# Block-diagonal w_phi for the two-block projections, and a new order of steps, in a fused linear-attention and FFN kernel

## The chip, the cores and the metric

The kernel runs on one core of a Trainium2 chip. The metric is device time in microseconds (us) of one execution; lower is better. A profile is of one execution, which has a time of its own; the time of the kernel is the median of several executions without a profile. TensorE is called PE in the profile, VectorE DVE, ScalarE ACT, GpSimd POOL and SyncE SP.

## What is computed

q, k and v have the shape (8, 8, 576, 64): batch, heads, positions, head size. w_phi is 64 x 128. Attention is linear, with a feature map of exponentials, and its output goes through a feed-forward network (FFN) with a squared relu.

```python
def phi(x):
    proj = einsum('bhsd,df->bhsf', x, w_phi)
    proj = proj - max(abs(proj), axis=-1, keepdims=True)
    return concatenate([exp(proj), exp(-proj)], axis=-1)
q_p, k_p = phi(q), phi(k)
kv = einsum('bhsf,bhsd->bhfd', k_p, v)
z = sum(k_p, axis=2)
num = einsum('bhsf,bhfd->bhsd', q_p, kv)
den = einsum('bhsf,bhf->bhs', q_p, z)[..., None] + 1e-06
x = (num / den).transpose(0, 2, 1, 3).reshape(4608, 512)
out = square(maximum(x @ w_in, 0)) @ w_out     # w_in 512 x 2048, w_out 2048 x 512
```

## The kernel before

The work is two streams that PE interleaves: the attention of eight batches, and the FFN of nine chunks of 512 tokens. Chunk c is the first 512 positions of batch c; chunk 8 collects the last 64 positions of every batch. An FFN chunk starts when the attention of its batch is done, and while PE works on it, the attention of the next batch goes on.

A batch's k and q are turned so that the head size lies on partitions (kT and qT), with two heads in the two halves of the 128 partitions: 18 blocks of 128 columns. Batches 0 and 1 are turned by PE (steps Txk, Txq), the later ones by transposing DMAs that SP issues (Xxk, Xxq, L339). Sixteen blocks come in groups of four; blocks 16 and 17, the last 64 positions, are a group of two, the group with index 4.

For a group, `project` (L347 to L360, matmuls at L355) multiplies each block by w_phi, once with the lower 64 partitions and once with the upper 64. These matmuls use half of the array's rows each, so two of them run side by side; they write to two PSUM banks. The steps are Pk for keys and Pq for queries. Then DVE takes the largest magnitude (Mk at L410, Mq at L517), and ACT the exponentials (L416). Queries of batches 0 to 4 are projected a second time in transposed form (Fq, L577), with w_phi as the stationary matrix, also in half-array form, and ACT writes their exponentials (L592). From batch 5 on (LATE), ACT takes them from Pq (L536) and a DMA turns them (Xf, L544). Batch 0 has forms of its own for Pk, most Pq and Fq (`first`, L382, L510).

V (L443, DVE) scales v by the key maxima's exponentials. KV (L473, L478) multiplies key features and v. NA and NB (L607) multiply query features and KV, with a scaling by DVE between (SA, L619); then come the reciprocal (L627), the division (xo, L631), and a transposing DMA to xT or xS (Xx, L665).

F1 (L751; f1 at L762 for chunk 0) is x @ w_in, one bank of 512 tokens and four matmuls at a time. relu (L726 on ACT or L728 on DVE) and the squaring (L735, DVE or POOL) follow. F2 (L816) adds four matmuls to an output tile of 128 tokens; after four parts the tile is copied (L196 or L198, "ot") and stored (L832, L835). The very last tile, token tile 3 of chunk 8, is done in two halves of 256 columns (`last_out`, L780, copies L794 and L796, stores L803).

The order is written out. Every step is an `Op` with a sequence number; the list `ORDER` gives the order in which all of them are emitted, and so the order on each engine and DMA queue, where work is strictly first come, first served. `BASES` gives each PSUM tile its bank, `STATES` chooses between two engines for the steps that have an alternative (relu, squaring, copies, V), `GATES` names for each load from batch 2 on a step that it has to wait for, and `FILL` puts matmuls on zeros ahead of some early steps (L885). Loads are issued by POOL (L254, L262, L274, L285, L301, L307). All these are fixed numbers in the file.

Of the kernel before, what the change touches and what calls it, by code (L numbers as in the profile page):

```python
# [111 lines left out]
def kernel(  # L112
# [10 lines left out]
    nc = tc.nc  # L123
# [4 lines left out]
    P = 128  # L128
# [34 lines left out]
    wphi2 = sb("wphi2", [Fd])  # L163
    ident = sb("ident", [P])
# [67 lines left out]
    add("DVE", dve_cost(64), f_wcast, r=[("wphi_f", 0), ("wphi_f", 1)], w=["wphi2"], what="wcast")  # L232

# [83 lines left out]
    def attention(b):  # L317
# [29 lines left out]
        def project(xt, ttag, ts, what):  # L347
            g = Bank(2, "att")
            n = len(ts)
# [9 lines left out]
            return g  # L359

# [6 lines left out]
        def kgroup_ops(g):  # L367
# [41 lines left out]
            def fn():  # L409
                pin(nc.vector.tensor_reduce(  # L410
                    out=mk_view(g), in_=ps2(pj)[:, :, : n * Fd].rearrange("p e (i f) -> p e i f", f=Fd),
                    axis=AX.X, op=ALU.max, apply_absolute_value=True))
            add("DVE", dve_cost(2 * n * Fd), fn, r=[pj], w=[pj] + [("mk", s2, g, e) for e in range(2)], what="Mk")
            for sgn, dst, nm in ((1.0, kp, "kp"), (-1.0, kn, "kn")):
                def fn(dst=dst, sgn=sgn):
                    pin(nc.scalar.activation(out=dst[slot][:, :, :n, :].rearrange("p e i f -> p e (i f)"),  # L416
                                             in_=ps2(pj)[:, :, : n * Fd], func=ACT.Exp, scale=sgn))
# [84 lines left out]
        def qmax_ops(c):  # L502
# [13 lines left out]
            def fn():  # L516
                pin(nc.vector.tensor_reduce(  # L517
                    out=mqb[:, c, :, :n], in_=ps2(pj)[:, :, : n * Fd].rearrange("p e (i f) -> p e i f", f=Fd),
                    axis=AX.X, op=ALU.max, apply_absolute_value=True))
            turned = b >= LATE  # L520
            add("DVE", dve_cost(2 * n * Fd), fn, r=[pj], w=[("mq", s2, c)] + [pj] * turned, closes=None if turned else pj, what="Mq")
            if turned:
# [6 lines left out]
                for u, sgn in enumerate((1.0, -1.0)):  # L529
                    def fn(u=u, sgn=sgn):  # L530
                        i_, o = ps2(pj)[:, :, : n * Fd], qe[:, u, : 2 * n * Fd]
                        if c == 4:
                            o, i_ = o.rearrange("p (i e f) -> p e i f", e=2, f=Fd), i_.rearrange("p e (i f) -> p e i f", f=Fd)
                        else:
                            o = o.rearrange("p (e x) -> p e x", e=2)
# [26 lines left out]
        def q_ops(c):  # L562
            ts = q_ts(c)
            n = min(len(ts), 4)
            pf = Bank(2, "att")
            def fn():
                o = ps2(pf)
# [11 lines left out]
            add("PE", pe_cost(1, 0.222 * n / 4 * (2 if first and c < 4 else 1)), fn,  # L579
                r=[("qT", s2, t) for t in ts] + ["wphi2"], w=[pf], opens=pf, tiled=True, what="Fq")  # L580
# [3 lines left out]
            for sgn, dst, nm in ((1.0, qp, "qp"), (-1.0, qn, "qn")):  # L584
                def fn(dst=dst, sgn=sgn):
                    i_ = ps2(pf)[:, :, : n * P]
# [447 lines left out]
```

## Time and profile before

| | |
|---|---|
| median of 3 runs | 350.82 us (350.69 to 351.57) |
| profiled execution | 351.74 us |
| its span, first to last instruction | 350.0 us |
| PE busy | 338.1 us, 97% |
| DVE busy | 277.3 us, 79% |
| ACT busy | 224.0 us, 64% |
| POOL busy | 96.7 us, 28% |
| granted clock of PE | 1.00 in every stretch |

Busy times of PE count a matmul from its start to a modelled end, and matmuls overlap: a 512-column one lasts 379 ns in the record, and the next starts 216 ns after it. So a matmul's cost is read from start to start. In the views of groups and waits, "L751 PE MATMUL psum<-xT,win" is line 751's matmul that writes psum and reads xT and win. In a timeline row the columns are the start, the length, the engine, the line, the operation, and how many instructions the row merges; what stands in brackets is idle time before it and what ended it. In a row of stretches, the busy time of each engine is followed by its number of instructions.

### The profile page before, as it was taken

To read this page: it belongs to the slowest core of one execution; us is meant where nothing else is said; L and a number is where in the kernel's file an instruction comes from. 1 tells how busy PE (TensorE), PEld (TensorE's weight loads), DVE (VectorE), ACT (ScalarE), POOL (GpSimd) and SP (SyncE) were. 2 spreads that over 40 slices of the span, in tenths; PEclk is the share of its full clock that TensorE was granted. 3 is DMA by queue.
4 is the path that set the end of the run, shared out by engine and by line. 5 is a ranking of instruction groups with operands and counts; after the bars stand their busy time and mean duration, and the time that the engine had idled before them with its cause. 6 is when DMAs were issued, how large, how long until landed. Compare 5 with 4: busy or idle time off the path is not lost.

```text
span 350.0 us, 8421 instructions
## 1 busy us (share of the span) xinstructions
PE 338.1 (97%) x3336; PEld 192.0 (55%) x3370; DVE 277.3 (79%) x530; ACT 224.0 (64%) x422; POOL 96.7 (28%) x144
## 2 busy tenths in 40 slices
PE   7889999999999999999999999999999999999995
PEld 5669976544654655465546544555546544444453
DVE  4999998899989997899998877988867737861421
ACT  4999886599779998785886776677537400122210
POOL 8744450298607143441100470220000000000000
PEclk9999999999999999999999999999999999999999
DMA  7999999799999999999997998979595621100024
GB/s 93 174 199 201 198 98 160 154 117 148 201 170 168 111 173 134 165 131 134 181 173 133 146 221 131 179 114 150 135 190 89 133 60 67 62 0 1 32 97 113
DMA packets 124328, 46.70 MB, mean 133 GB/s; under 512 B 92800, under 2 KB 119808, under 8 KB 124288
## 3 DMA queue, kind: packets, MB, share of 16 engines
q0 software_dynamic: 45216, 18.36, 47.2%
q1 hardware_dynamic: 78752, 27.50, 41.0%
q8 instruction: 26, 0.43, 0.5%
q10 hardware_dynamic: 320, 0.30, 0.4%
q14 instruction: 14, 0.11, 0.1%
HBM read 36.77 MB, written 9.44 MB: 132 GB/s over the span
## 4 chain that ended last, share of the span: by engine, by line
PE 81%; DVE 10%; DMA 4%; issue 3%; ACT 2%; POOL 0%; DVEq 0%; ACTq 0%; POOLq 0%
PE psum L751 30%; PE psum L816 29%; PE psum L607 5%; PE psum L355 5%; PE psum L473 4%; PE psum L762 3%; DVE va L443 2%; DMA xT<-xo 2%; DMA xq<-in_q_dram 2%; DVE mq L517 2%; PE psum L577 1%; DVE mk L410 1%; DVE mk L389 1%; PE psum L780 1%; PE psum L478 1%
## 5 line engine op out<-in xcount | busy, mean ns | idle before, releaser
L816 PE MATMUL psum<-wout,h 128*128 128x512 bf16 x526 | 129.3, 379 | 2.1 <-issue 0.5
L751 PE MATMUL psum<-xT,win 128*128 128x512 bf16 x448 | 106.3, 379 | 0.7 <-DMA xT<-xo 0.7
L726 ACT ACTIVATE hr<-psum 128x512 bf16<-128x512 f32 x88 | 51.4, 599 | 51.7 <-PE psum L751 28.4
L816 PEld LDWEIGHTS <-h 128*128 128x128 bf16 x560 | 51.1, 98 | 54.9 <-issue 1.0
L751 PEld LDWEIGHTS <-win 128*128 128x128 bf16 x512 | 47.3, 98 | 54.5 <-issue 1.8
L735 DVE TENSOR_TENSOR h<-hr 128x512 bf16<-128x512 bf16 x143 | 55.7, 414 | 8.5 <-ACT hr L726 8.1
L592 ACT ACTIVATE qf<-psum 128x1024 bf16<-128x1024 f32 (+1 forms) x50 | 45.5, 936 | 11.4 <-PE psum L577 7.2
L517 DVE TENSOR_REDUCE mq<-psum 128x8 f32<-128x1024 f32 (+1 forms) x40 | 44.0, 1109 | 3.2 <-PE psum L355 2.8
L728 DVE TENSOR_SCALAR hr<-psum 128x512 bf16<-128x512 f32 x56 | 37.6, 685 | 9.4 <-PE psum L751 7.6
L410 DVE TENSOR_REDUCE mk<-psum 128x8 f32<-128x1024 f32 (+1 forms) x35 | 38.4, 1111 | 5.7 <-PE psum L355 5.3
L416 ACT ACTIVATE kp<-psum 128x1024 bf16<-128x1024 f32 (+1 forms) x35 | 32.6, 936 | 7.8 <-DVE mk L410 7.8
L607 PEld LDWEIGHTS <-qf 128*128 128x128 bf16 x640 | 28.2, 97 | 13.1 <-issue 0.9
L619 DVE TENSOR_TENSOR psum<-psum,en 128x520 f32<-128x520 f32 (+1 forms) x40 | 27.6, 699 | 6.6 <-PE psum L607 4.9
L416 ACT ACTIVATE kn<-psum 128x1024 bf16<-128x1024 f32 (+1 forms) x35 | 32.5, 939 | 0.0
L607 PE MATMUL psum<-kv,qf 128*128 128x65 bf16 x640 | 31.3, 193 | 0.1
L443 DVE TENSOR_TENSOR va<-xv,va 64x256 bf16<-64x256 bf16 (+2 forms) x68 | 30.2, 463 | 0.8 <-ACT va L435 0.2
L198 ACT ACTIVATE ot<-psum 128x512 f32<-128x512 f32 x21 | 12.5, 596 | 26.8 <-PE psum L816 26.5
L254 POOL DMA_DIRECT2D xk<-in_k_dram x28 | 20.5, 733 | 32.3 <-ACT qf L592 8.9
L631 DVE TENSOR_TENSOR xo<-psum,rden 128x512 bf16<-128x512 f32 (+1 forms) x40 | 27.3, 686 | 0.8
L274 POOL DMA_DIRECT2D xq<-in_q_dram x24 | 17.1, 718 | 39.1 <-DVE h L735 17.6
L254 POOL DMA_DIRECT2D xv<-in_v_dram x26 | 19.0, 741 | 24.8 <-ACT en L551 22.9
L196 DVE COPY ot<-psum 128x512 f32<-128x512 f32 x14 | 9.6, 685 | 19.0 <-PE psum L816 17.4
(68 smaller groups left out, 384.5 us busy)
## 6 DMA issues: line engine op xcount, KB each, us to landing
out_dram<-ot SPq DMA_DIRECT2D x32, 256.0 KB, 2.7
xk<-in_k_dram POOLq DMA_DIRECT2D x26, 128.0 KB, 4.2
xq<-in_q_dram POOLq DMA_DIRECT2D x24, 128.0 KB, 6.4
xv<-in_v_dram POOLq DMA_DIRECT2D x24, 128.0 KB, 4.9
win<-in_moe_w_in_dram POOLq DMA_DIRECT2D x4, 512.0 KB, 11.7
wout<-in_moe_w_out_dram POOLq DMA_DIRECT2D x4, 512.0 KB, 12.2
xq<-in_q_dram POOLq DMA_DIRECT2D x4, 256.0 KB, 6.2
xv<-in_v_dram POOLq DMA_DIRECT2D x2, 512.0 KB, 9.8
```

The costliest lines, as they stand in the source:

```text
L254: pin(nc.gpsimd.dma_start(out=x[:, a * 512 : z * 512].rearrange("p (h x) -> p h x", x=4 * D), in_=src[b][2 * a : 2 * z, 0:512, :].rearrang ...
L410: pin(nc.vector.tensor_reduce(out=mk_view(g), in_=ps2(pj)[:, :, : n * Fd].rearrange("p e (i f) -> p e i f", f=Fd), axis=AX.X, op=ALU.max, ...
L416: pin(nc.scalar.activation(out=dst[slot][:, :, :n, :].rearrange("p e i f -> p e (i f)"), in_=ps2(pj)[:, :, : n * Fd], func=ACT.Exp, scale= ...
L443: pin(engine().tensor_tensor(out=t[:, :, :D].rearrange("p m (x c) -> p m x c", c=2), in0=x.rearrange("p (m x c) -> p m x c", m=n, c=2), in ...
L517: pin(nc.vector.tensor_reduce(out=mqb[:, c, :, :n], in_=ps2(pj)[:, :, : n * Fd].rearrange("p e (i f) -> p e i f", f=Fd), axis=AX.X, op=ALU ...
L592: pin(nc.scalar.activation(out=o, in_=i_, func=ACT.Exp, scale=sgn))
L607: pin(nc.tensor.matmul(out=o[:, u // 4, u % 4 * D1 : (u % 4 + 1) * D1], lhsT=(qp, qn)[sg][slot][:, u * m : u * m + P], rhs=kv_sb[s2][:, h ...
L726: pin(nc.scalar.activation(out=hr[sl], in_=ps1(g), func=ACT.Relu))
L728: pin(nc.vector.tensor_scalar(out=hr[sl], in0=ps1(g), scalar1=0.0, scalar2=None, op0=ALU.max))
L735: pin(engine().tensor_tensor(out=dst, in0=i_, in1=i_, op=ALU.mult))
L751: pin(nc.tensor.matmul(out=o, lhsT=win[mc // 4][:, kc, mc % 4 * P : (mc % 4 + 1) * P], rhs=x, start=(kc == 0), stop=(kc == KC - 1)))
L816: pin(nc.tensor.matmul(out=ps1(g), lhsT=h2[c % 2][mc // 4][:, mc % 4, tt * P : (tt + 1) * P], rhs=wout[mc // 4][:, mc % 4, :], start=(mc = ...
```

## The change

A new tile `wbd` of 128 x 256 holds w_phi twice: in rows 0 to 63 of columns 0 to 127, and in rows 64 to 127 of columns 128 to 255; the rest is zero. Groups of two blocks multiply all 128 rows by it, so that one matmul gives both heads' projections side by side in one bank. This holds for Pk of batches 1 to 7, Pq of all batches, and the transposed Fq of batches 1 to 4, whose two matmuls use the two halves of wbd as the stationary matrix. Three steps are new (3, 4, 5), so that every later step's number is raised by 3: old step 692 is new step 695.

```diff
+    wbd = sb("wbd", [2 * Fd])
...
+    def f_wbd0():
+        pin(nc.vector.memset(wbd, 0.0))
+
+    add("DVE", (0.14, 0.3), f_wbd0, w=[("wbd", 0), ("wbd", 1)], what="wbd0")
+    for e in range(2):
+        def fn(e=e):
+            pin(nc.vector.tensor_copy(out=wbd[64 * e : 64 * e + 64, e * Fd : e * Fd + Fd], in_=wphi_f[64 * e : 64 * e + 64, :]))
+        add("DVE", dve_cost(64), fn, r=[("wphi_f", e)], w=[("wbd", e)], what="wbd")
...
         def project(xt, ttag, ts, what):
+            n = len(ts)
+            if n == 2:
+                g = Bank(1, "att")
+                def fn():
+                    for i, t in enumerate(ts):
+                        pin(nc.tensor.matmul(out=ps1(g)[:, 2 * i * Fd : 2 * (i + 1) * Fd], lhsT=xt[:, t, :], rhs=wbd, start=True, stop=True))
+                add("PE", pe_cost(n, 0.1075), fn, r=[(ttag, s2, t) for t in ts] + [("wbd", 0), ("wbd", 1)], w=[g], opens=g, what=what)
+                return g
             g = Bank(2, "att")
-            n = len(ts)
...
+        def projected(g, n):
+            if g.size == 1:
+                return ps1(g).rearrange("p (i e f) -> p e i f", e=2, f=Fd)
+            return ps2(g)[:, :, : n * Fd].rearrange("p e (i f) -> p e i f", f=Fd)
...
-            pf = Bank(2, "att")
-            def fn():
+            small = c == 4 and not first
+            pf = Bank(1 if small else 2, "att")
+            def fn():
+                if small:
+                    for u in range(2):
+                        pin(nc.tensor.matmul(out=ps1(pf)[:, 256 * u : 256 * u + 256].rearrange("f (i x) -> f i x", x=P),
+                                             lhsT=wbd[:, u * Fd : u * Fd + Fd], rhs=qTb[:, 16:18, :], start=True, stop=True))
+                    return
```

The reductions and exponentials of these groups read the one bank through `projected`, in the same number of elements.

The lists are new. Up to list place 208 `ORDER` is the old one with the new steps put in (3 behind the first clearing of va, 4 and 5 ahead of the first transposes); from there on it is a different order. `BASES`, `GATES` and 101 of the 275 entries of `STATES` differ too; `FILL` is the same up to the numbers. Lines of it to which the text refers, the old order first:

```diff
-    482, 609, 725, 465, 780, 726, 709, 466, 595, 483, 448, 484, 603, 486, 487, 613, 467, 596, 610, 761, 604, 488,
-    616, 449, 608, 731, 489, 618, 490, 735, 762, 739, 491, 615, 614, 485, 597, 492, 493, 605, 607, 964, 743, 692,
...
-    1509, 1385, 1367, 1266, 1386, 1401, 1399, 1432, 1541, 1406, 1267, 1545, 1400, 1268, 1519, 1419, 1433, 1434, 1420,
-    1414, 1403, 1421, 1085, 1443, 1523, 1549, 1245, 1405, 1550, 1527, 1257, 1513, 1336, 1514, 1269, 1480, 1422, 1277,
...
+    7, 6, 0, 1, 8, 3, 12, 16, 18, 2, 9, 15, 11, 4, 5, 17, 43, 13, 44, 14, 10, 45, 67, 47, 46, 22, 68, 49, 21, 69, 48,
...
+    182, 34, 193, 212, 358, 345, 351, 194, 230, 352, 348, 356, 213, 501, 42, 359, 231, 195, 353, 240, 183, 505, 196,
+    33, 184, 354, 214, 357, 232, 509, 244, 197, 233, 257, 267, 360, 248, 242, 280, 215, 185, 256, 259, 361, 281, 241,
+    208, 383, 380, 364, 268, 362, 243, 198, 266, 282, 367, 381, 382, 247, 246, 209, 245, 251, 258, 368, 513, 250,
...
+    434, 603, 582, 483, 586, 597, 720, 587, 461, 484, 465, 485, 486, 724, 604, 605, 466, 728, 487, 729, 591, 467,
+    489, 752, 770, 490, 589, 468, 469, 583, 598, 712, 612, 606, 592, 774, 599, 756, 491, 593, 616, 610, 488, 607,
+    760, 492, 734, 493, 613, 611, 470, 600, 615, 738, 627, 494, 742, 608, 775, 746, 495, 618, 601, 619, 496, 609,
+    643, 621, 659, 629, 772, 776, 650, 747, 764, 644, 651, 765, 652, 779, 699, 646, 703, 634, 700, 626, 620, 695,
...
+    1277, 1346, 1386, 1387, 1354, 1388, 1269, 1406, 1371, 1490, 1508, 1494, 1088, 1270, 1534, 1398, 1389, 1434, 1271,
+    1401, 1356, 1422, 1339, 1435, 1512, 1540, 1436, 1279, 1248, 1498, 1373, 1423, 1516, 1424, 1260, 1425, 1439, 1272,
+    1544, 1400, 1499, 1402, 1408, 1548, 1280, 1357, 1491, 1437, 1281, 1375, 1500, 1407, 1487, 1282, 1495, 1426, 1438,
...
+    1723, 1725, 1727, 1644, 1679, 1662, 1703, 1713, 1726, 1728, 1692, 1704, 1696, 1680, 1729, 1707, 1730, 1731, 1714,
+    1708, 1709, 1705, 1697, 1710, 1733, 1698, 1715, 1732, 1712, 1716, 1717, 1711, 1719, 1718,
```

More of the change, by code (lines that the diff above doesn't have):

```diff
@@ L415, in fn @@
                 def fn(dst=dst, sgn=sgn):
[L416 to L417 removed]
+                    o, i_ = dst[slot][:, :, :n, :], projected(pj, n)
+                    if n == 4:
+                        o, i_ = o.rearrange("p e i f -> p e (i f)"), i_.rearrange("p e i f -> p e (i f)")
+                    pin(nc.scalar.activation(out=o, in_=i_, func=ACT.Exp, scale=sgn))
                 add("ACT", act_cost(2 * n * Fd), fn, r=[pj], w=[pj] + [(nm, slot, e) for e in range(2)],
@@ L578, in fn @@
                                          lhsT=wphi2[r, :], rhs=rhs, start=True, stop=True))
-            add("PE", pe_cost(1, 0.222 * n / 4 * (2 if first and c < 4 else 1)), fn,
-                r=[("qT", s2, t) for t in ts] + ["wphi2"], w=[pf], opens=pf, tiled=True, what="Fq")
+            add("PE", pe_cost(1, 0.215 if small else 0.222 * n / 4 * (2 if first and c < 4 else 1)), fn,
+                r=[("qT", s2, t) for t in ts] + ([("wbd", 0), ("wbd", 1)] if small else ["wphi2"]), w=[pf], opens=pf, tiled=not small, what="Fq")
             slot = qslot[0] % NQP
@@ L585, in fn @@
                 def fn(dst=dst, sgn=sgn):
-                    i_ = ps2(pf)[:, :, : n * P]
+                    i_ = ps1(pf).rearrange("f (e y) -> f e y", e=2) if small else ps2(pf)[:, :, : n * P]
                     if c == 4:
```

28 lines of the change are left out of this document (14 added, 14 removed), and 171 rows, old and new, of tables (GATES, ORDER).

## The prediction

> **What bounds the kernel now.** The page comes first: which engine is full, and what the chain that ended last is made of.
>
> ```profile
> span 350.0 us, 8421 instructions
> PE 338.1 (97%) x3336; PEld 192.0 (55%) x3370; DVE 277.3 (79%) x530; ACT 224.0 (64%) x422; POOL 96.7 (28%) x144
> PE 81%; DVE 10%; DMA 4%; issue 3%; ACT 2%; POOL 0%; DVEq 0%; ACTq 0%; POOLq 0%
> ```
>
> TensorE is the bound, so a gain must shorten its own work, fill a hole in it, or shorten what follows its last matmul. The view of stretches says where holes are.
>
> ```profile
> 0.00:28.00 28.00, 23.70 (x320) 17.86 (x320) 22.15 (x50) 22.06 (x51) 19.28 (x31) 1.00 1.26 158
> 28.00:46.00 18.00, 17.95 (x323) 15.80 (x325) 17.36 (x37) 16.27 (x31) 6.58 (x10) 1.00 1.39 197
> 46.00:130.00 84.00, 82.46 (x951) 47.47 (x962) 77.39 (x143) 69.94 (x132) 38.70 (x57) 1.00 1.14 150
> 130.00:200.00 70.00, 69.24 (x713) 37.53 (x715) 63.40 (x114) 53.35 (x98) 20.63 (x31) 1.00 1.07 149
> 200.00:290.00 90.00, 88.96 (x781) 46.54 (x789) 69.81 (x133) 51.73 (x96) 11.51 (x17) 1.00 0.79 139
> ```
>
> The first number is the stretch, the second PE's busy time, then weight loads, DVE, ACT, POOL. The first 28 us lose 4.3, but the order up to list place 208 (about 35 us) is the old one, with only the three new steps put in. From 28 to 290 us PE is idle 0.05 + 1.54 + 0.76 + 1.04 = 3.4 us. That is the most the new order can win in waits; some matmul records are missing from the trace, so part of it is not idle at all. The view of waits for PE names few of them in this stretch, and the timeline prices those from start to start, since a matmul's end is modelled; the bracket is the idle time and its releaser.
>
> ```profile
> 108.80 0.59 PE L751 MATMUL psum<-xT,win 128*128 128x512 bf16 x2
> 109.75 0.61 PE L751 MATMUL psum<-xT,win 128*128 128x512 bf16 x2 [0.36 <-DMA xT<-xo]
> ...
> 255.49 0.59 PE L751 MATMUL psum<-xT,win 128*128 128x512 bf16 x2
> 256.43 0.59 PE L751 MATMUL psum<-xT,win 128*128 128x512 bf16 x2 [0.35 <-DMA xT<-xo]
> ...
> 49.20 1.03 PE L816 MATMUL psum<-wout,h 128*128 128x512 bf16 x3
> 50.63 0.19 PE L473 MATMUL psum<-va,kp 128*128 128x65 bf16 x1 [0.40 <-DVE va L443]
> ...
> 182.70 0.39 PE L355 MATMUL psum<-wphi,qT 64*128 64x128 bf16 x8
> 183.30 0.19 PE L473 MATMUL psum<-va,kp 128*128 128x65 bf16 x1 [0.21 <-DVE hr L728]
> ```
>
> A 512-column matmul takes 0.216 us in an unbroken run (82.50 to 86.90 below: 20 of them and one change of array form). Two took 0.95 and 0.94, so the two waits for the transposed output cost 0.52 and 0.51: **1.03 us**. The third place holds four F2 matmuls (three recorded), 0.86 of 1.43: 0.57 lost. The fourth holds eight small blocks, 0.32 (70.69 to 71.01, below) of 0.60: 0.28 lost. Together 0.85 behind VectorE.
>
> **The change, part by part.** *(a) The new matmuls.* Nineteen groups change: Pk of batches 1 to 7, Pq of batches 0 to 7, Fq of batches 1 to 4. Batch 0's own Pk and Fq stay.
>
> ```profile
> 70.34 0.29 PE L355 MATMUL psum<-wphi,kT 64*128 64x128 bf16 x4
> 70.46 0.39 PE L355 MATMUL psum<-wphi,qT 64*128 64x128 bf16 x8
> 70.69 0.39 PE L355 MATMUL psum<-wphi,kT 64*128 64x128 bf16 x8
> 71.01 1.04 PE L816 MATMUL psum<-wout,h 128*128 128x512 bf16 x4
> ...
> 82.50 4.48 PE L751 MATMUL psum<-xT,win 128*128 128x512 bf16 x20
> 86.90 0.40 PE L355 MATMUL psum<-wphi,qT 64*128 64x128 bf16 x8
> ...
> 117.57 0.41 PE L607 MATMUL psum<-kv,qf 128*128 128x65 bf16 x8
> 117.91 0.40 PE L355 MATMUL psum<-wphi,qT 64*128 64x128 bf16 x8
> 118.15 0.38 PE L577 MATMUL psum<-qT,wphi 64*128 64x512 bf16 x2
> ...
> 119.33 0.41 PE L607 MATMUL psum<-kv,qf 128*128 128x65 bf16 x8
> 119.58 0.59 PE L751 MATMUL psum<-xT,win 128*128 128x512 bf16 x2
> ...
> 344.61 1.47 PE L780 MATMUL psum<-wout,h 128*128 128x256 bf16 x12
> ```
>
> Four half-array blocks took 0.12 (70.34 to 70.46). A full-array matmul over 256 columns takes 0.109: the last row, 12 of them, less 0.27 for the end of one, over 11 steps. Two are 0.22. So each group costs 0.10 to 0.11 more: **+2.0 us** for 19.
>
> *(b) Changes of array form.* Eight L607 matmuls are followed after 0.34 by a half-array group and after 0.25 by a full one: entering costs 0.09. Eight half-array blocks last 0.23 to 0.24 when another such group follows, 0.32 before a full one: leaving costs 0.09. I walked both orders through PE's steps, fillers as full, and counted each change: 116 in the old, 96 in the new (58 runs of half-array groups become 48). Twenty fewer at 0.09: **-1.8 us**. The old order with the new matmuls would have 108, so most of this is the new order's doing. (a) and (b) make **+0.2**.
>
> The Trainium skill, "TensorEngine Tiling (Array Packing)", Tiling Modes, says that changing the tiling mode drains TensorE; the 0.09 us rows agree. Its Performance Considerations would keep row tiling wherever the contraction is 64 or less, for up to twice the speed: by that alone the change is a loss, the +2.0 of (a), and the row of 0.12 against 0.22 agrees.
>
> *(c) The three new VectorE steps.* A memset, then two casts behind the cast of w_phi.
>
> ```profile
> 3.02 0.23 DVE L230 CAST wphi<-wphi_f 128x128 bf16<-128x128 f32 x1 [1.67 <-DMA wphi_f<-in_w_phi_dram]
> 3.25 0.56 DVE L246 MEMSET va<- 128x264 uint32 x2
> 5.15 0.42 DVE L196 COPY kT<-psum 128x512 bf16<-128x512 bf16 x1 [1.34 <-PE psum L329]
> ```
>
> The memset falls into the 1.67 of waiting; it writes half as much as one of the two memsets that take 0.56. The casts (0.23 at most, half the partitions of the first) fall into the 1.34 before 5.15. Cost **0**; without that cover, up to 0.7.
>
> *(d) The waits.* Places are given in us of PE work, summed down each list at the durations above. The first F1 group of chunk 2 stands in the old order 6.4 us of PE work behind the last NB that feeds it (step 482, then six F2, two Pk, one Fq, NA and NB, then 692). In the new one the last such NB is 467, with eight F2, two Pk, three Fq, one Pq, NA and NB up to 699: 9.1 us. For chunk 6, 1266 to 1480 has seven F2 and two Pq, 6.7; 1269 to 1491 has ten F2, two Pq and an NA, 9.5. Each gains 2.7 us or more against a wait of 0.5. For the other chunks the distances are 9.5, 14.2, 9.8, 8.2, 6.5 and 11.2; the 6.5 (chunk 7) is unchanged and had no wait.
>
> ```profile
> DMA to landing us min/median/max: 2.3/3.2/7.1
> ```
>
> That is the transpose at L665, median 3.2 from issue. Both waits go: **-1.0**. The bounds are 0, if the queue is slower there, and -1.03.
>
> For the waits behind VectorE (0.85, and about 0.3 in places under 0.2) the order alone doesn't tell; bounds 0 and -1.15. What speaks for a gain is VectorE's load.
>
> ```profile
> L735 DVE TENSOR_TENSOR h<-hr 128x512 bf16<-128x512 bf16 x143 | 55.7, 414 | 8.5 <-ACT hr L726 8.1
> L728 DVE TENSOR_SCALAR hr<-psum 128x512 bf16<-128x512 f32 x56 | 37.6, 685 | 9.4 <-PE psum L751 7.6
> ```
>
> By the two lists of alternatives (STATES) twelve squarings go from DVE to POOL (12 x 0.414 = 5.0) and six relu to ACT (6 x 0.685 = 4.1); five output copies come to DVE, which read PSUM as a relu does (3.4). About 5.7 us of 277.3 go. I take half of the waits: **-0.55**.
>
> *(e) POOL.* Thirteen squarings where one was, and one V, in the queue that also issues the loads.
>
> ```profile
> 80.67 1.04 POOL L735 TENSOR_TENSOR h<-hr 128x512 bf16<-128x512 bf16 x1 [1.06 <-DVE hr L728]
> DMA to landing us min/median/max: 6.9/12.2/13.2
> ```
>
> Six stand at list places worth 28 to 39 us of PE work. Behind the fifth (351) is the last quarter of w_out (42), listed at 36.5 to 37.3; its first F2 (513) starts at 43.2: a distance of 5.9 to 6.7. In the old order it was 7.7. The second row is the landing of the four w_out loads: at least 6.9. The cost is 0 if it lands as the order needs, 1.0 at 6.9, and 5.5 to 6.3 at the median of 12.2. Few loads stand ahead of it in the new list, so I stay near the fastest: **+0.2**.
>
> *(f) The end.*
>
> ```profile
> 343.08 0.60 ACT L198 ACTIVATE ot<-psum 128x512 f32<-128x512 f32 x1 [4.37 <-PE psum L816]
> 343.70 2.93 SPq L832 DMA_DIRECT2D out_dram<-ot  x4
> 346.12 0.42 DVE L794 COPY otl<-psum 128x256 f32<-128x256 f32 x1 [0.62 <-PE psum L780]
> 346.72 0.55 SPq L803 DMA_DIRECT2D out_dram<-otl  x1
> ```
>
> The old order ends with a 256-column half (otl, 0.42, issue 0.55). The new ends with a whole group of token tile 2: F2 1712 and 1716, then ot 1717 on ACT (0.60) and a store issue of 0.73 (2.93 over 4). That is 0.18 + 0.18 more, less up to 0.15 because SP was busy to 346.63 in the old and is freer now: **+0.25**, bounds 0 and 0.4.
>
> The sum: +0.2 + 0 - 1.0 - 0.55 + 0.2 + 0.25 = **-0.9 us**. The profiled execution took 351.74, 1.74 outside its span, and would take 350.8. It was 0.92 above the median of the three runs shown; from 350.82 the forecast is **349.9 us**.
>
> **The rivals.** *The waits only move* (R1): (d) saves the 1.0, the waits behind VectorE return elsewhere, and (e) costs up to 0.7; the sum is -0.35 to +0.15, 350.5 to 351.0. For it speaks that PE is full, so each removed wait leaves the same number of waiting steps.
>
> *POOL holds the loads* (R2, slower): the squarings put w_out, and behind it the second half of batch 1's q (33), late. It decides when w_out needs over 6.7 us from its issue; at the old load's median of 12.2 PE waits 5.5 to 6.3, and 356 us is its far end. Later, batch 3's k transpose is listed at 73.0 and its first Pk at 83.9: 10.9 us, where the old order had 16.0 (71.3 and 87.3). At 2 to 3 us of lateness in one of these places the time is 352 to 353.
>
> *All waits go* (R3): (d) at its bound with no new wait: +0.2 + 0.25 - 2.2 = -1.75, 349.1; with the end at 0 and every hole of 28 to 290 us filled, 347.6.
>
> *The narrow part alone* (R4): the new matmuls do what they say, but the form changes cost less than 0.09 inside a full queue, say half: then (b) is -0.9 and all becomes 350.8.
>
> **How the numbers follow.** Forecast (349.4 to 350.3) 0.38, R1 and R4 0.22, R2 0.22, R3 0.18. About 0.3%, 1.05 us, is what a measurement here can tell from no change: 349.77 and 351.87 are the borders. The forecast lies 0.1 inside the first, and its cases fall on both sides: half to faster. With R3 that gives faster 0.40; same 0.38 (the other half, R1, R4, and a little of R2); slower 0.22. The range takes in R3 to 348.6, R2 to 353.0, and leaves out the far ends of both.
>
> **What would show it.** L355 and L577 with 128 rows, 19 groups at 0.22 instead of 0.12, and 96 changes of form. No wait of L751 for xT at the first groups of chunks 2 and 6. PE's idle time between 28 and 290 us under 2.5 us instead of 3.4. The last matmul of L816, not L780, then an ACT copy. I am wrong if L816, L329 or L355 waits for a load between 40 and 60 us or near 90, or if PE's idle time after 28 us grows.

## The result and the profile after

The change made the kernel slower: 355.75 us (median of 4, 353.85 to 356.43) against 350.75 us for the kernel before beside it (4 runs), a ratio of 1.0127 with a 95% interval of 1.0105 to 1.0148. The forecast was 349.9 us, in a range of 348.6 to 353.0: wrong in sign and outside the range. The profiled execution after took 355.68 us. Now and then a run is longer than the others of its kernel; in the set of a_both2, b_fill and bn_loads5 below, five of the 29 runs of the kernel before took 352.8 to 354.8 us, so the ratios there lie lower than the medians tell.

The first lines of the page of the kernel after, and the chain that ended last:

```profile
span 353.9 us, 8415 instructions
PE 340.5 (96%) x3340; PEld 193.1 (55%) x3340; DVE 275.7 (78%) x516; ACT 226.1 (64%) x426; POOL 112.9 (32%) x157
PE 78%; DVE 9%; DMA 6%; ACT 3%; issue 2%; POOL 0%; DVEq 0%; ACTq 0%; POOLq 0%; SPq 0%
```

VectorE and TensorE do about what they did; POOL does 16 us more. DMA rose from 4 to 6% of the chain and TensorE fell from 81 to 78: time went into waits, not into work. The view of stretches (length, then PE's busy time) and the view of waits for PE say where:

```profile
28.00:46.00 18.00, 17.77 (x307) 15.55 (x304) 17.46 (x35) 15.87 (x28) 13.03 (x16) 1.00 1.22 171
46.00:130.00 84.00, 81.31 (x943) 47.39 (x941) 75.37 (x129) 67.83 (x129) 43.96 (x58) 1.00 1.04 142
130.00:200.00 70.00, 69.84 (x690) 37.49 (x688) 62.47 (x114) 54.11 (x102) 23.86 (x35) 1.00 1.19 160
200.00:290.00 90.00, 88.69 (x790) 46.35 (x788) 70.63 (x132) 53.29 (x98) 12.96 (x19) 1.00 0.80 141
```

```profile
PE psum L372 <- ACT hr L756: 1.6, 1, 1.6
PE psum L781 <- DMA xT<-xo: 1.5, 2, 1.3
...
PE psum L497 <- DVE va L467: 0.6, 1, 0.6
PE psum L846 <- DVE ot L197: 0.5, 1, 0.5
```

Between 28 and 290 us PE is idle for 0.23 + 2.69 + 0.16 + 1.31 = 4.4 us, where it was 3.4 and I forecast under 2.5. For prices I set each TensorE step's start against the work listed up to it, at the prediction's durations. Work: 334.60 us before, 334.74 after. Waiting after 28 us: 4.3 before, 8.15 after. From the last matmul's start to the end: 4.2 before, 4.9 after. (Before's profile was also 0.7 later at 28 us, in code that did not change.) By these sums the spans agree: +0.14 of work, +3.85 of waits and +0.7 at the end, less the 0.7 that the profile before had lost earlier, make the 3.9 us between 350.0 and 353.9. The large new waits, from start to start, are 1.72 us at step 446 (84 us), 0.74 at step 435 (96 us, a KV that waits for a V step), 1.49 at the first F1 of chunk 5 (212 us) and 0.71 at step 1713 (341 us).

**The wait at 84 us, followed back.** The timeline of the kernel after (start, time, engine, line; the bracket is idle time before it and its releaser):

```profile
78.06 5.07 POOL L765 TENSOR_TENSOR h<-hr 128x512 bf16<-128x512 bf16 x4 [0.48 <-DVE hr L758]
...
79.05 1.74 DVE L467 TENSOR_TENSOR va<-xv,va 64x256 bf16<-64x256 bf16 x2
79.37 1.42 DVE L467 TENSOR_TENSOR va<-xv,va 128x1024 bf16<-128x1024 bf16 x1
...
81.31 0.92 DVE L467 TENSOR_TENSOR va<-xv,va 128x1024 bf16<-128x1024 bf16 x1
...
82.16 1.26 DVE L765 TENSOR_TENSOR h<-hr 128x512 bf16<-128x512 bf16 x1
...
83.45 1.09 ACT L756 ACTIVATE hr<-psum 128x512 bf16<-128x512 f32 x2 [2.00 <-DVE h L765]
...
84.10 0.40 PE L372 MATMUL psum<-wphi,qT 64*128 64x128 bf16 x8 [1.55 <-ACT hr L756]
```

Read it from the bottom. PE waits for a PSUM bank that a ReLU on ACT must empty; the ReLU waits 2.00 us for an hr buffer; the buffer is read by a squaring on VectorE, which takes 1.26 us and stands behind V steps that take 1.42 and 0.92. All lie beside four squarings on POOL. (A merged row shows the shape of its first instruction only: of the two V steps from 79.05, 1.74 us together, the first has 64x256 and takes 0.30; the second has 128x1024. Its row stands below the merged one, from a narrower window.) The same view with VectorE undisturbed is shown under the second experiment. The groups by line give the extremes (min, median, max in ns):

```profile
L765 DVE TENSOR_TENSOR h<-hr x131: 365/418/1257, 34.1 to 335.6; 128x512 bf16<-128x512 bf16 x131
L765 POOL TENSOR_TENSOR h<-hr x13: 1039/1072/1482, 32.8 to 94.5; 128x512 bf16<-128x512 bf16 x13
...
L467 DVE TENSOR_TENSOR va<-xv,va x67: 271/409/1893, 17.6 to 266.8; 64x256 bf16<-64x256 bf16 x32, 128x1024 bf16<-128x1024 bf16 x27, 128x512 bf16<-128x512 bf16 x8
```

Before, the maxima on VectorE were 427 and 693. In the profile after, six VectorE instructions with both inputs in SBUF are longer than usual beside a step on POOL, by 0.1 to 1.2 us each and 3.3 together; ReLUs and reductions, which read PSUM, keep their 0.68 and 1.21 us beside it. The Trainium skill, "SBUF — State Buffer", Who interferes with whom, has the rule: a VectorE instruction with two SBUF inputs contends with a GpSimd instruction that reads SBUF, and the one that comes second is blocked. The rows agree that they contend, and one pair with the order: a V step of 0.69 us was ahead of a squaring, which then took 1.25. Another pair does not: the V step at 94.20 starts ahead of a squaring of usual length and takes 1.89.

```profile
92.27 0.69 DVE L467 TENSOR_TENSOR va<-xv,va 128x1024 bf16<-128x1024 bf16 x1
92.59 1.25 POOL L765 TENSOR_TENSOR h<-hr 128x512 bf16<-128x512 bf16 x1 [1.46 <-ACT hr L756]
...
94.20 1.89 DVE L467 TENSOR_TENSOR va<-xv,va 128x1024 bf16<-128x1024 bf16 x1
94.49 1.05 POOL L765 TENSOR_TENSOR h<-hr 128x512 bf16<-128x512 bf16 x1
```

**The end.** The last steps of the kernel after:

```profile
342.35 7.07 PE L846 MATMUL psum<-wout,h 128*128 128x512 bf16 x32
```

```profile
349.50 0.60 ACT L199 ACTIVATE ot<-psum 128x512 f32<-128x512 f32 x1 [4.63 <-PE psum L846]
350.13 0.50 ACTq L862 DMA_DIRECT2D out_dram<-ot  x1
```

As forecast, a whole F2 group and an ACT copy end it. From the last matmul's start to the last store's issue it takes 1.09 us instead of 0.91, and from there to the end 3.77 instead of 3.28: a 128 KB store ends it where a 64 KB one did.

### The profile page after: what moved, and what is told of

It is laid out like the page before. It is cut to its first block, busy times and chain, and to the rows that moved or that the text cites. A ratio compares the mean times of both kernels' runs of the same rounds, so it can differ in the third digit from the quotient of the medians.

```text
span 353.9 us, 8415 instructions
## 1 busy us (share of the span) xinstructions
PE 340.5 (96%) x3340; PEld 193.1 (55%) x3340; DVE 275.7 (78%) x516; ACT 226.1 (64%) x426; POOL 112.9 (32%) x157
## 4 chain that ended last, share of the span: by engine, by line
PE 78%; DVE 9%; DMA 6%; ACT 3%; issue 2%; POOL 0%; DVEq 0%; ACTq 0%; POOLq 0%; SPq 0%
PE psum L846 30%; PE psum L781 28%; PE psum L637 5%; PE psum L792 4%; PE psum L497 4%; PE psum L372 3%; DVE va L467 3%; DMA xT<-xo 3%; DVE mq L541 2%; DMA xq<-in_q_dram 2%; PE psum L607 1%; DMA out_dram<-ot 1%; ACT hr L756 1%; ACT qf L622 1%; DVE mk L411 1%
## 5 line engine op out<-in xcount | busy, mean ns | idle before, releaser
L846 PE MATMUL psum<-wout,h 128*128 128x512 bf16 x560 | 133.2, 379 | 0.5 <-DVE ot L197 0.5
L756 ACT ACTIVATE hr<-psum 128x512 bf16<-128x512 f32 x94 | 53.8, 598 | 66.0 <-PE psum L781 57.9
L765 DVE TENSOR_TENSOR h<-hr 128x512 bf16<-128x512 bf16 x131 | 52.9, 424 | 11.3 <-ACT hr L756 10.7
L758 DVE TENSOR_SCALAR hr<-psum 128x512 bf16<-128x512 f32 x50 | 33.8, 684 | 12.0 <-PE psum L781 11.3
L467 DVE TENSOR_TENSOR va<-xv,va 64x256 bf16<-64x256 bf16 (+2 forms) x67 | 31.6, 493 | 1.3 <-ACT va L453 0.7
L197 DVE COPY ot<-psum 128x512 f32<-128x512 f32 x19 | 13.1, 689 | 16.3 <-PE psum L846 12.4
L497 PE MATMUL psum<-va,kp 128*128 128x65 bf16 x256 | 19.6, 193 | 1.3 <-DVE va L467 0.6
```

The source lines that it names most:

```text
L467: pin(engine().tensor_tensor(out=t[:, :, :D].rearrange("p m (x c) -> p m x c", c=2), in0=x.rearrange("p (m x c) -> p m x c", m=n, c=2), in ...
L756: pin(nc.scalar.activation(out=hr[sl], in_=ps1(g), func=ACT.Relu))
L758: pin(nc.vector.tensor_scalar(out=hr[sl], in0=ps1(g), scalar1=0.0, scalar2=None, op0=ALU.max))
L765: pin(engine().tensor_tensor(out=dst, in0=i_, in1=i_, op=ALU.mult))
L846: pin(nc.tensor.matmul(out=ps1(g), lhsT=h2[c % 2][mc // 4][:, mc % 4, tt * P : (tt + 1) * P], rhs=wout[mc // 4][:, mc % 4, :], start=(mc = ...
```

## The experiments

Each ran beside the kernel before, whose median was 350.75 to 350.94 us in every set. What stands in brackets behind a time is the ratio to it, with its 95% interval. The new order's squarings on GpSimd are called the late seven (78 to 95 us in the profile after) and the early six; with them goes step 250, a V step.

**1. All squarings back** (a_nopool). The 13 squarings and step 250 on VectorE:

```diff
 STATES, the 14 groups of steps 250, 327, 333, 336, 342, 351, 357, 500, 504, 512, 522, 526, 558, 566
-1
+0
```

> The changed kernel, with its thirteen squarings and the one V on GpSimd put back on VectorE at the same places of the list; nothing else differs. Theory (GpSimd holds VectorE): while a squaring runs on GpSimd, a VectorE instruction with both inputs in SBUF runs long (64x256 V 1.42 us where 0.28 is usual, 128x1024 V 1.89 where 0.68 is usual), and PE's waits at 84.1 (1.72 us), 96.2 (0.74) and 52.7 us (0.49) follow from it. Then most of these 2.9 us go: 353.0 to 354.0 us. Rival (the new order itself is late there, and VectorE is too full): VectorE gets about 6 us of work back, the waits stay or grow: 355.5 to 357 us.

355.96 us (1.0139, 1.0113 to 1.0164): no gain, as the rival had it. (The 1.42 us of the expectation belong to the 128x1024 V step, 0.68 where it is undisturbed.) No VectorE squaring exceeds 428 ns now, so the hold-ups are gone, and with them the waits at 96 and 341 us; the one at 84 falls to 1.23. But VectorE is full early: the lag that the kernel after had at 72 us, 7.57, is 9.35 here, through waits of 0.50 at 40 us and 1.02 at 53 (0.49 in the kernel after). Without GpSimd's early steps other waits come.

**2. The late seven back** (a_late), the early six left on GpSimd:

```diff
 STATES, the 7 groups of steps 500, 504, 512, 522, 526, 558, 566
-1
+0
```

> The kernel after with seven of its thirteen GpSimd squarings (those that run from 69 to 95 us: steps 500, 504, 512, 522, 526, 558, 566) given back to VectorE; the six early ones and step 250 stay on GpSimd. Theory A (a squaring on GpSimd holds up the VectorE instruction beside it, and these hold-ups reach TensorE at 84 and 96 us): the VectorE copies of V beside them fall from 0.9-1.9 to 0.3-0.7 us, the wait of 1.72 us at step 446 falls to about 1.2 (what it was with all thirteen back) and that of 0.74 at step 435 to under 0.2, and the time is about 354.7 us. Theory B (VectorE has no room there for the squarings either): the waits of 2.5 us change places but keep their sum, and the time stays at 355.7.

354.14 us (1.0093, 1.0062 to 1.0123), 1.6 under the kernel after, though the intervals overlap. The timeline of VectorE in this kernel, at the place shown above:

```profile
79.02 0.29 DVE L467 TENSOR_TENSOR va<-xv,va 64x256 bf16<-64x256 bf16 x1
79.34 0.42 DVE L765 TENSOR_TENSOR h<-hr 128x512 bf16<-128x512 bf16 x1
79.68 0.68 DVE L467 TENSOR_TENSOR va<-xv,va 128x1024 bf16<-128x1024 bf16 x1
...
81.81 1.09 DVE L765 TENSOR_TENSOR h<-hr 128x512 bf16<-128x512 bf16 x3
```

VectorE does four more squarings here between 79.3 and 82.8 us, and its next ReLU still starts 0.5 us sooner (82.82 instead of 83.34). Theory A holds: the wait at 84 us falls to 1.24 and the one at 96 goes, though 0.52 comes at step 474. The 1.24 that stay are not GpSimd's: they stand with no squaring on GpSimd too (a_nopool).

**3. The same steps on GpSimd in the old order** (b_pool).

```diff
 STATES of the kernel before, the groups of the same 14 steps
-0
+1
```

> The kernel before, with the same steps on GpSimd as in the changed kernel: fourteen more GpSimd steps (its own one squaring stays), the order unchanged. Theory (GpSimd holds VectorE): VectorE's instructions with two SBUF inputs run long beside them and PE waits: 1.5 to 3 us slower than before, 352.3 to 353.8 us. Rival (VectorE is the shortage and is relieved of 6 us): 350.0 to 351.0 us.

363.04 us (median of 4, 362.10 to 368.25; 1.0334, 1.0307 to 1.036): 12 us slower, where the theory gave 1.5 to 3, so both expectations missed. PE's waits in this kernel:

```profile
PE psum L751 <- DVE hr L728: 1.8, 1, 1.8
PE psum L816 <- POOL h L735: 1.5, 1, 1.5
PE psum L355 <- ACT hr L726: 1.1, 1, 1.1
...
PE psum L473 <- POOL va L443: 0.8, 1, 0.8
```

Here PE waits for results of GpSimd itself (1.5 and 0.8 us); for the kernel after the view lists no such wait. So the old order needs them sooner than GpSimd has them. How much of the 12 us is this, and how much are hold-ups of VectorE, was not taken apart.

**4. More buffers for hr** (a_hr6, and later a_both_hr5).

```diff
-    hr = ring("hr", 4, [TCH])
+    hr = ring("hr", 6, [TCH])
```

> The kernel after with a ring of six buffers for the ReLU result hr in place of four, nothing else. Theory A (TensorE's wait of 1.72 us at step 446, at 84 us, is a ReLU on ScalarE that stands for a free hr buffer, because the squaring that reads the buffer is late on VectorE; with two more buffers the ReLU runs at once and gives up its PSUM bank): the wait falls below 0.5 us, ScalarE's idle time of 2.00 us before that ReLU goes, and the time is about 354.4 us. Theory B (VectorE's own queue is the limit: what it owes is only asked for later): the wait shows up again within some 15 us at another step fed by VectorE, and the time stays within 0.4 us of 355.7.

356.96 us (1.0184, 1.0132 to 1.0235). The wait at step 446 goes, but VectorE's delay shows at other steps: 0.89 at 85 us, 0.85 at 97, 0.73 at 48; waiting between 72 and 140 us is 3.2 us where it was 3.8. Theory B is nearer. These two kernels and the one with four ot buffers do not give the same output as the others; they are used for their waits alone.

**5. SyncE's queue** (a_sp): a store and a transpose of the last block put behind chunk 5's four transposes.

```diff
 ORDER
-    1107, 1061, 1151, 1142, 1133, 1138, 1062, 1185, 891, 1049, ... 1143, 1156, 1075, 1039, 1147,
+    1107, 1061, 1151, 1133, 1138, 1062, 1185, 1049, ... 1143, 1156, 1075, 1039, 1142, 891, 1147,
```

> The changed kernel, with one store (1142) and the xS transpose (891) moved in SyncE's queue from ahead of the four xT transposes of batch 5 to behind them; nothing else differs. Theory (queue order): the four issues start 1.75 us earlier and PE's wait of 1.5 us at 211.8 us goes: 354.2 to 354.6 us. Rival (the transposes land late because loads share the DMA engines at 203 to 210 us): the wait stays at 1 us or more, 355.2 to 355.9 us.

355.59 us (1.0125, 1.0107 to 1.0144). The transposes are issued from 199.8 to 204.4 us instead of 203.3 to 207.1, and F1 still waits 1.29 us: this theory falls. Issued 3 us sooner, one of them still takes 6.8 us to land.

**6. The loads beside the transposes** (a_loads): four 128 KB loads put behind the ReLU of chunk 5's first group, in place and gate.

```diff
 ORDER: 1358, 1372, 1359 and 1361 taken out, and
-    1209, 1294, 1295, 1290,
+    1209, 1294, 1295, 1358, 1372, 1359, 1361, 1290,
 GATES
-    1358: 1078, 1359: 1015, 1361: 1187, 1372: 1081
+    1358: 1295, 1359: 1295, 1361: 1295, 1372: 1295
```

> The kernel after with four 128 KB input loads on GpSimd's queue (steps 1358, 1359, 1361 of k and 1372 of v, issued at 202 to 205 us) put behind step 1295, the ReLU of the first group of chunk 5, some 9 us later, by their place in the order and by their gates. Theory A (the four transposes of xT for chunk 5 land 6 us after their issue because the loads' packets share the DMA engines with them): they land 3 to 4 us after issue, the wait of 1.49 us at step 1294 falls below 0.4, the time is about 354.4 us. Theory B (they land late for a reason of their own, the queue of SyncE or the stores beside them): the wait stays at 1.2 to 1.5 and the time at 355.7. Theory C: the loads, 9 us late, make the next batch's first transposes wait, and what is gained at 212 us is lost before 235.

354.49 us (1.0096, 1.0059 to 1.0134). The view of the tile xT from 200 to 214 us, first in the kernel after, then in this one:

```profile
L695 SPq DMA_TRANSPOSE xT<-xo x4: 1203/1214/1275, 203.3 to 207.1; - x4
...
DMA to landing us min/median/max: 4.5/5.2/6.5
```

```profile
L695 SPq DMA_TRANSPOSE xT<-xo x4: 1202/1214/1258, 202.1 to 206.0; - x4
...
DMA to landing us min/median/max: 2.3/2.3/2.4
```

Same transposes, same issue times within 1.2 us: 5.2 us to land beside the loads, 2.3 without. The wait of 1.49 us is gone. Theory A. The median is 1.3 under the kernel after; the intervals overlap.

**7. A fourth ot buffer on top** (a_loads_ot4).

```diff
-    ot = ring("ot", 3, [DM], F32)
+    ot = ring("ot", 4, [DM], F32)
```

> As the run with the four loads behind step 1295, and a ring of four output buffers ot in place of three. Theory A (the wait of 0.71 us at step 1713, at 341 us, is a copy into ot that stands for the store of the buffer three groups before): it goes, and the time is 0.7 us below that of the run with the loads alone. Theory B (the copy is late because ScalarE is, the store being only the last in the list of what it waits for): the wait stays, and the two runs agree within 0.3 us.

354.38 us (1.0091, 1.006 to 1.0121). In the kernel after the copy that empties the bank waited for an old store, and PE for the copy:

```profile
340.31 0.69 DVE L197 COPY ot<-psum 128x512 f32<-128x512 f32 x1 [3.71 <-DMA out_dram<-ot]
```

With four buffers that wait goes (0.62 us in the run with the loads alone), but the medians differ by 0.1 only, so its worth is not shown. The wait is also absent in a_late.

**8. Both edits** (a_both: 2 and 6 together), with **five hr buffers** (a_both_hr5), and with **a milder hold** (a_both2: the four loads behind step 1315, near 208 us, instead of 1295).

> The kernel after with both edits that helped: the four loads behind step 1295, and the seven late squarings back on VectorE. Theory A (the two waits are separate causes): the gains add, 1.3 us for the loads and 1.6 for the squarings, so about 352.9 us, and what is left above the kernel before is the wait at step 446 (1.2), the end (0.7) and the creep of small waits. Theory B (what one edit frees the other loses, since TensorE is full and waits only move): no better than either alone, 354.0 to 354.5.

> As the run with both edits, and five buffers for the ReLU result hr in place of four. Theory A (once VectorE is rid of the hold-ups, the 1.24 us left at step 446 are the ReLU that stands for an hr buffer): the wait falls below 0.6 us, the time is 0.6 to 1.2 us under that of the run with both edits. Theory B (as with six buffers before, the wait goes to the next step that VectorE feeds, within 15 us): the sum of the waits between 72 and 140 us stays within 0.3 us and so does the time.

> The kernel after with the seven late squarings on VectorE and the four loads held back less far, behind step 1315 (about 208 us) in place of step 1295 (211 us). Theory A (holding the loads cost at 227 us, where the next batch's k then came late, 0.92 us, what it gained at 212): both waits stay under 0.5 us, and the median is 353.0 to 353.6. Theory B (some other transfer is late in its turn, from run to run): the median stays at 354.1, with a spread of 2 us or more.

a_both: 354.12 us (1.009, 1.0066 to 1.0114), no better than one edit alone: the held loads made the next batch's k late.

```profile
226.95 0.39 PE L363 MATMUL psum<-wbd,kT 128*128 128x256 bf16 x2 [0.76 <-DMA kT<-xk]
```

a_both2: 353.49 us (12 runs; 1.0063, 1.0037 to 1.0089), 2.3 under the kernel after and below its interval. Its stretch from 200 to 290 us has no hole:

```profile
200.00:290.00 90.00, 90.00 (x797) 47.13 (x796) 71.32 (x132) 53.81 (x100) 12.91 (x19) 1.00 0.80 142
```

So both edits together gain more than either by the medians, 2.3 us against 1.6 and 1.3, though less than their sum, and the intervals of the three overlap. a_both_hr5 took 356.46 us (1.0155, 1.0138 to 1.0173): the wait at 446 goes, a 0.89 comes at 84, and waits of 0.3 to 0.9 stand at seven later places. Neither theory had that: as in theory B the wait only moves, but the time rises by 2.3.

**9. The narrow part alone** (b_narrow): the new matmuls and their three steps in the old order, with the old gates and banks.

```diff
 ORDER, GATES, BASES, STATES of the kernel before, every step from 3 on numbered 3 higher
+ steps 3, 4, 5 at the places that they have in the kernel after
```

> The new matmuls alone: the old order, banks, engines and gates, with the block-diagonal matmuls in the nineteen groups and the three new VectorE steps. By the count of the forecast: nineteen groups at 0.105 us more are +2.0, eight fewer changes of array form (116 to 108) at 0.094 are -0.75, together +1.2: 351.8 to 352.2 us. Rival (the freed bank, or form changes that cost less inside a full queue, decide): 350.6 to 351.2 us, or over 352.5 us.

353.97 us (1.0104, 1.0068 to 1.0141): the rival's upper branch. By the list its work is 1.27 us more (the 2.0 of 19 dearer groups, less 8 changes of form); the median is 3.2 more. In the profile, its fastest run, the other cost is PE's wait at chunk 2:

```profile
110.80 0.60 PE L781 MATMUL psum<-xT,win 128*128 128x512 bf16 x2 [1.13 <-DMA xT<-xo]
```

1.30 us from start to start, against 0.54 before, though the transposes were issued in the same tenths of a microsecond.

**10. Loads held in the old order**, without the new matmuls (b_loads) and with them (b_narrow_loads: chunk 2's; bn_loads5: chunk 5's too, by gating step 1361 on 1155).

```diff
 ORDER: 964, 773, 962, 770, 772 behind step 693; GATES of these five
+    693
```

> The kernel before with the five input loads on GpSimd's queue that are issued from 105 to 109 us (steps 962, 964, 770, 772, 773) put behind step 693, the ReLU of the first group of chunk 2, by place and by gate. Theory A (a wait for xT is set by the loads in flight beside the transposes, and not by how much TensorE work stands between, as the forecast had it): the wait of 0.54 us at chunk 2 goes without any change of TensorE's order, and the time is 350.2. Theory B (the distance in TensorE work sets it): the wait stays at 0.4 to 0.6 and the time at 350.8. Theory C: the loads, some 5 us late, are missed by batch 3's first transposes near 130 us, and the time is 351 to 353.

> The kernel before with the new matmuls and their three new VectorE steps in the old order, and with the same five loads put behind the ReLU of the first group of chunk 2. Theory A (the new matmuls' own cost is the 1.3 us of added TensorE work, and the other 0.8 of its profile, up to 1.9 of its median, is the wait for xT at chunk 2 beside those loads): the wait of 1.30 us goes to under 0.4 and the time is 352.0 to 352.9. Theory B (the new matmuls cost more than their work all along the kernel): the time stays at 353.6 to 354.2.

> The kernel before with the new matmuls and the five loads near 105 us held back, and now also the train of loads that ran from 203 to 209 us gated on step 1155 (near 208 us), behind the issue of chunk 5's four transposes. Theory A (what is left of the new matmuls' cost is the chance of a wait at chunk 5, 1.97 us in one profile and none in another, when the transposes share the DMA engines with these loads): no wait over 0.4 for xT at 212 us, the median is 352.2 to 353.0 and the runs spread by under 1.5 us. Theory B (the cost lies elsewhere): the median stays at 353.8 to 354.4 and the runs go on spreading by 2 to 3 us.

b_loads: 350.74 us (0.9996, 0.9985 to 1.0007), no change in time. But the wait for xT at chunk 2 is gone. Its transposes' landing, before and in b_loads, and the first F1 group of chunk 2 in b_loads with what follows:

```profile
DMA to landing us min/median/max: 2.4/2.6/4.3
```

```profile
DMA to landing us min/median/max: 2.4/2.4/2.6
```

```profile
107.86 1.03 PE L751 MATMUL psum<-xT,win 128*128 128x512 bf16 x4
...
109.94 0.40 PE L355 MATMUL psum<-wphi,qT 64*128 64x128 bf16 x8 [0.29 <-ACT kn L416]
```

The four matmuls run in a row now; in their place PE loses 0.21 and 0.46 us at the two projections behind them, the second to ScalarE. So the loads do set the wait for xT, as theory A had it, and still the time stays: PE waits at the next steps for what is late there. b_narrow_loads: 354.14 (1.009, 1.0065 to 1.0114); again the wait for xT at chunk 2 goes, 0.70 and 0.47 come behind ScalarE in its place, and chunk 5 now waits 1.97 us. bn_loads5: 353.83 (12 runs; 1.0063, 1.0033 to 1.0092); chunk 5 no longer waits, but ScalarE does, for the transposes of qf, and behind it a ReLU and then PE for 2.03 us:

```profile
223.81 1.94 ACT L560 ACTIVATE xk<-psum 128x1024 bf16<-128x1024 f32 x2 [3.76 <-DMA qf<-xk]
```

Both theories A were right about the wait that they named and wrong about the time.

**11. What of the new matmuls costs this** (b_fill, b_pad, bn_end; a_both2_end).

```diff
 b_fill: FILL of the kernel before, 12 idle matmuls in the unused half of a bank
+    209: (2, 1, 256), 313: (6, 1, 256), ... 1270: (2, 1, 256), 1467: (0, 1, 256)
 b_pad
-    warm = sb("warm", [256])
+    warm = sb("warm", [512])
 bn_end and a_both2_end: wbd = sb("wbd", [2 * Fd]) moved behind otl
```

> The kernel before, all its steps and their order unchanged, with 12 idle full-array matmuls of 248 columns (0.106 us each, 1.27 us in all, results read by nobody) put one each ahead of 12 of the two-block projections. It gives TensorE the same added work as the new matmuls give it in the old order (1.27 us), and nothing else of them. Theory A (the 3.2 us of the new matmuls in the old order are 1.3 of work, and the rest is what any small delay of this order sets off in the transposes): the median is 353 to 354, and its runs spread by over 2 us. Theory B (an order that is late by 1.3 us is only late by 1.3 us; the rest belongs to the new matmuls' own form or bank): the median is 351.8 to 352.4, with a spread like that of the kernel before (1.5).

> The kernel before with 512 unused bytes per partition put behind its small constants, so that every later tile (inputs, their transposes, qf, xT, hr, h, ot) lies 512 bytes higher, as the new tile wbd makes it in the kernel after. No instruction, order or gate changes. Theory A (the 1.9 us of the new matmuls' cost that added TensorE work does not explain are the 512 bytes: at the new addresses the transposes land later): the median is 352.4 to 353.2 and the runs spread by over 2 us. Theory B (addresses do not matter): 350.6 to 351.1, as before.

> The kernel before with the new matmuls in the old order (the run of the narrow part alone), the tile wbd given its place behind all other tiles, so that these lie where they lay before the change; nothing else differs from that run (353.97 us). Theory A (addresses): the median falls to 351.8 to 352.4, that of the run with idle matmuls of the same work, and the spread to about 1. Theory B: it stays at 353.5 to 354.4 with runs 2 to 3 us apart.

> The kernel after with the seven late squarings on VectorE, the four loads held back behind step 1315 (353.49 us so far), and the tile wbd placed behind all other tiles. Theory A (addresses): about 1.9 us come off, 351.4 to 351.9, and the runs come closer together. Theory B: 353.2 to 353.8, as without the move.

b_fill: 351.86 us (12 runs, 351.49 to 352.47; 1.0011, 0.9984 to 1.0039). Added TensorE work of 1.27 us costs 1.0 by the medians, and nothing is set off. b_pad: 350.74 (1.0, 0.9986 to 1.0014) and bn_end 353.44 (1.0076, 1.0054 to 1.0098): an effect of addresses is not seen. a_both2_end: 353.61 (1.0078, 1.0054 to 1.0102), as a_both2. So 1.5 to 2.3 us of the new matmuls' cost in the old order, by the medians of the four kernels that have them, is neither their work nor the place of their tile. What the profiles show is where it falls. The issue of chunk 5's transposes from SyncE (min, median, max in ns, first and last start), in before, b_fill, b_narrow and b_narrow_loads:

```profile
L665 SPq DMA_TRANSPOSE xT<-xo x4: 1193/1258/1454, 197.1 to 201.7; - x4
```

```profile
L665 SPq DMA_TRANSPOSE xT<-xo x4: 1189/1226/1259, 197.4 to 201.9; - x4
```

```profile
L695 SPq DMA_TRANSPOSE xT<-xo x4: 1190/1239/2231, 199.2 to 204.1; - x4
```

```profile
L695 SPq DMA_TRANSPOSE xT<-xo x4: 1190/1235/3462, 199.3 to 205.4; - x4
```

All four profiles with the new matmuls in the old order start these transposes 1.3 to 3.2 us later than the four with the old matmuls. But TensorE is late by as much there. The same F1 group, before and in b_narrow:

```profile
200.87 1.89 PE L751 MATMUL psum<-xT,win 128*128 128x512 bf16 x8
```

```profile
202.92 1.89 PE L781 MATMUL psum<-xT,win 128*128 128x512 bf16 x8
```

In the four it starts 1.5 to 2.2 us later than before, and the first of the transposes 1.6 to 2.2: the late start is what the added work and earlier waits had cost by then. What comes on top is one issue of 2.0 to 3.5 us, where none in the other four took over 1.46. In each of the four profiles the cost beyond work is seen as waits: for xT at chunk 2 (1.30, 1.21) or behind ScalarE in its place, and later for transposes (1.97, 2.03, 0.73 us, or none). From 28 us on, b_narrow's profile loses 2.2 us on that of the kernel before: 1.27 by work, 0.76 at chunk 2, the rest in small parts. The waits differ from profile to profile, and the runs of a kernel spread by 2 to 3 us. Why one issue is long, and why one transpose of chunk 2 took 5.3 us to land in b_narrow where the slowest took 4.3 before, stays open; whether the matmuls' full-array form or their one bank matters was not taken apart.

## Why the prediction was wrong, point by point

*(a) and (b), the matmuls.* Right: the kernel after has 38 matmuls over 128 rows (16 + 14 + 8), 19 groups of two. One pair, with the next step's start:

```profile
73.20 0.38 PE L363 MATMUL psum<-wbd,qT 128*128 128x256 bf16 x2
73.41 1.89 PE L781 MATMUL psum<-xT,win 128*128 128x512 bf16 x8
```

0.21 us, as priced. Total work came out 0.14 higher, where +0.2 was forecast. R4 fell: in both profiles four matmuls of F1 or F2 take 0.86 us before a full-array step and 0.96 before a half-array one, so a change of form costs its 0.09 in a full queue too.

*(c)* Right: no wait came of the three steps.

*(d), first half.* The waits at the first groups of chunks 2 and 6 went, as counted. The step that failed is to book that as the sum, "Both waits go: -1.0": 1.49 and 0.38 came in their place. I judged the other chunks by TensorE work between the last NB and the first F1, and by a landing time of 3.2 us. In the new order chunk 5's transposes fell beside four loads, took 5.2 and cost 1.49; 0.38 came at chunk 1. The distance did not tell: summed the same way, chunk 5's is 7.6 us in the old order, where it did not wait, and 8.2 in the new. A landing time belongs to what else moves at that moment, which the list of the queues would have told.

*(d), second half, and (e).* These failed most. "I take half of the waits: -0.55" counted on VectorE's 5.7 us of relief; its busy time fell by 1.6 (277.3 to 275.7). The squarings on GpSimd held up VectorE's own steps with both inputs in SBUF, and gave part of the relief back: 0.7 us on one V step (79.37 us, 1.42 instead of 0.68), 1.2 on another (94.20, 1.89 instead of 0.68), 0.8 on a squaring (82.16, 1.26 instead of 0.42). The +0.2 of (e) priced them as entries in a queue of loads, and no wait for w_out came; that they could hold VectorE had no term. Taking seven of them back was worth 1.6 by the medians. The profile before could not have told: beside its single squaring on GpSimd (80.67 us) VectorE ran ReLUs and a reduction, which read PSUM, at their usual length.

*(f)* +0.25 forecast, +0.67 measured in the profile: the longer copy was right (0.18); the last issue took 0.50 and not the 0.73 of the sum, and from its start to the end it took 0.5 longer, which was not counted. (The last two F2 are steps 1715 and 1716; 1712 is a store.) The wait of 0.71 us for an ot buffer at 341 us was not foreseen.

*The rivals.* R1 (waits only move) named what happened but let the sum rise to +0.15 at most; waits between 28 us and the last matmul grew by 3.9. R2 had the sign and the wrong place: no load held TensorE near 43 or 84 us.

The bill, by the medians: 5.0 us slower, of which 2.3 are GpSimd's late squarings and the loads beside chunk 5's transposes, shown by taking both away at once (a_both2; its interval lies below that of the kernel after). About 2.6 stay. In the profile of a_both2 the largest are 1.24 at step 446, 0.9 at steps 427 and 474 and the 0.7 of the end; against them the waits of 0.54, 0.51 and 0.28 of the kernel before are gone. What causes these is open: the new order with the old matmuls was not run, so how much is the order's and how much the new matmuls', as in the old order, is not shown. No version beat the kernel before.

## What to carry to other kernels

Before moving elementwise work to GpSimd, list what VectorE does beside it: a VectorE instruction with both inputs in SBUF took up to 1.2 us longer beside a GpSimd squaring of 1.04, and a full TensorE had no room for that. When an order is changed, check each transpose's landing against the loads that are issued within 5 us of it, not against a median. A wait that goes at one place in a full pipeline is a gain only if the sum of waits falls: in b_loads it went, and the time stayed.

## What was not expected of the hardware

A 128x512 squaring on GpSimd took 1.04 us alone and up to 1.48 beside VectorE; a 128x1024 V step on it 1.96, where VectorE takes 0.68. Four xT transposes landed in 2.3 us each with no load of GpSimd's queue beside them and in 4.5 to 6.5 us with four 128 KB loads. The issue of one xT transpose held SyncE 1.2 us as a rule, and up to 3.5 us.
